# A ranking emitted six wide products later, and the last expert's scatter-adds without an order among them

## The chip, the cores and the metric

The kernel runs on one core of a Trainium2 chip. Its engines are TensorE (PE in the profile; PEld is its weight load), VectorE (DVE), ScalarE (ACT), GpSimd (POOL) and SyncE (SP), and 16 DMA engines. The metric is the device time of one execution in microseconds.

## The reference

Three layers follow each other on 3072 tokens of 384 numbers: a linear attention with decay, a product of two linear maps with two more maps behind it, and a mixture of eight experts of which each token takes two.

```python
for t in range(S):                                   # attention: 4 x 8 heads, 768 steps, 48 wide
    state = alpha[:, :, t, :, None] * state + np.einsum('bhd,bhe->bhde', k[:, :, t], v[:, :, t])
    y[:, :, t] = np.einsum('bhd,bhde->bhe', q[:, :, t], state)
...
h = (x @ w1) * (x @ w2) @ w3                         # x: 3072 x 384, w1, w2: 384 x 1024
x = h @ w_out
...
noisy_logits = x @ w_gate + np.log1p(np.exp(x @ w_noise)) * noise
top2 = np.argpartition(-noisy_logits, 2, axis=1)[:, :2]
for e in range(E):                                   # 8 experts, 384 -> 1024 -> 384
    for k in range(2):
        mask = top2[:, k] == e
        h = np.maximum(x[mask] @ w1[e], 0.0)
        out[mask] += top2_w[mask, k, None] * (h @ w2[e])
```

## The kernel before

**Groups.** The tokens are worked on in eight groups g of 384. For a group the kernel does, in turn, the attention in three chunks, the wide products of the second layer, the narrow products, and the routing. w3 and w_out are multiplied into one matrix beforehand (`Wf`). Factors are held as two half-precision parts, "h" and "l", so a product is three matmuls a block: h by h, h by l, l by h.

**Wide and narrow products.** `wide(g, f, i)` forms block f (of eight) of x @ w1 or x @ w2 (i is 0 or 1): nine matmuls on L531 to L533. ScalarE copies the result (ab), VectorE multiplies the two (L539) and splits the product into gh and gl (L180, L182). So a group has 16 wide products. `narrow(g, t, part)` multiplies gh and gl by `Wf` and the gates (L555 to L557), for three blocks t of 128 tokens in two parts each.

**Attention beside it.** Its steps are woven between these products: scores (L299) with scales of their own (L275 to L289), a mask and a split (sf on L306, sm on L180 and L182, the latter on GpSimd), the mix with the state (L338, L349), the state's own update (L368 on TensorE, Zs on L392 and L393 on VectorE), the turns of the output (ys, L401) and of the inputs (pad, L219), Qt and Kt (L246, L261).

**Routing and ranking.** `route(g, ...)` runs on VectorE and ScalarE behind the narrow products of group g and ends with M, which marks each token's two experts, and the counts of the tokens ahead (M on L644 and L646, R on L647, md on L639 to L641). `rank(g)` turns M into places: two small matmuls (L656, L657), some ten short operations on VectorE (rk on L659 to ad on L682), and six indirect DMAs on GpSimd (L685), which write the tokens' numbers and weights into a table in memory. The first ranking also starts the filling of the output with zeros (`clear`).

**Experts.** Behind the last group each expert e gathers its tokens by the table, takes them through its two layers (L894 to L905, L911 to L916) and adds the results to the output: `put` scales a tile of 128 tokens on ScalarE (ysb, L934) and GpSimd issues an indirect DMA that adds its rows in memory (L935), seven for an expert.

**What sets the order.** TensorE runs in the order in which the program emits its instructions. A loop takes units from two lists, the attention's and `mix_units`, by their costs. On the other engines a scheduler sets the order ahead of time, by when it expects operands. In `mix_units` the ranking of group g-1 is emitted in group g behind block f = RF = 3, that is behind eight wide products. PSUM is used in eight buffers in rotation, one also for each ranking. Two DMAs that touch the same tensor are ordered by a wait unless the program declares that they don't depend on each other; `rank` does so for the table's.

Of the kernel before, what the change touches and what calls it, by code (L numbers as in the profile page):

```python
# [20 lines left out]
P = 128  # L21
# [3 lines left out]
E = 8  # L25
# [5 lines left out]
NG = NTOK // G  # L31
# [8 lines left out]
NTA = G0 // P  # L40
NFR = 2
RF = 3
PA = 1
WB = 12
WU = 3
# [39 lines left out]
def body(ctx, tc, q, k, v, alpha, mw1, mw2, mw3, mwo, wg, wn, noise, ew1, ew2, out, dbg=None):  # L85
    nc = tc.nc
# [678 lines left out]
    def fuse_units():  # L765

        n0 = 4 * NK
        yield 0.33, (lambda: fuse_out_turn(0)), n0 + 1
        for f in range(NF):
            if f + 1 < NF:  # L770
                yield 0.33, (lambda f=f: fuse_out_turn(f + 1)), n0 + f + 2
            yield 0.55, (lambda f=f: fuse_out(f)), 0
        n0 += NF
        seq = [(f, hf) for f in range(NF) for hf in range(2)]
        yield 0.45, (lambda: fuse_turn(*seq[0])), n0 + 1
        for n, x in enumerate(seq):
            if n + 1 < len(seq):
                yield 0.45, (lambda n=n: fuse_turn(*seq[n + 1])), n0 + n + 2
            yield 2.05, (lambda x=x: fuse_mul(*x)), 0
# [16 lines left out]
    def mix_units():  # L796
        fu = fuse_units()
        for g in range(NG):
            for f in range(NF):
                for i in range(2):  # L800
                    if g == 0:
                        yield (0.0, (lambda f=f: convert((f // 4 + 1) * 2 * NK + AH)), TG - 1)
                    yield (1.48, (lambda g=g, f=f, i=i: wide(g, f, i)), (g + 1) * TG - 1)
                    if g == NG - 1 and f > RF:
                        yield (0.0, (lambda: prepare_after(LAST[-1], PA)), 0)
                    if g == 0 and f >= FF:
                        c, x, n = next(fu)
                        yield 0.0, (lambda n=n: convert(n + AH)), 0
                        yield c, x, 0
                if f == RF and g:  # L810
                    yield (0.1, (lambda g=g: LAST.append(rank(g - 1))), 0)
                    if g == NG - 1:
                        yield (0.0, begin_experts, 0)
            if g == 0:
                for c, x, n in fu:
                    yield 0.0, (lambda n=n: convert(n + AH)), 0
                    yield c, x, 0
                yield (0.0, end_of_weights, 0)
            for t in range(TG):
                for part in range(2):  # L820
                    yield (2.05, (lambda g=g, t=t, part=part: narrow(g, t, part)), 0)
                    if g == NG - 1:
                        yield (0.0, (lambda: prepare_after(LAST[-1], PA)), 0)
                        if 0 <= t * 2 + part - T0 < NTP[0]:
                            yield (0.34, (lambda i=t * 2 + part - T0: turn_part(0, 0, i)), 0)
# [78 lines left out]
        nc.scalar.activation(hh[:, f], pm, AF.Relu)  # L904
        nc.vector.scalar_tensor_tensor(hl[:, f], pm, 0.0, hh[:, f], op0=OP.max, op1=OP.subtract)  # L905

    def layer2(w2h, w2l, hh, hl, c0, n, mt, wv, t, midway=None):
        ts = slice(c0, c0 + n)
        py = bank(DM)
        for f in range(NF):  # L910
            nc.tensor.matmul(py[:n], hh[:, f, ts], w2h[:, f], start=f == 0, stop=False)  # L911
            nc.tensor.matmul(py[:n], hh[:, f, ts], w2l[:, f], start=False, stop=False)  # L912
            nc.tensor.matmul(py[:n], hl[:, f, ts], w2h[:, f], start=False, stop=f == NF - 1)  # L913
            if f == 2 and midway:
                midway()
        put(py[:n], n, mt, wv, t)  # L916

    def layer2t(w2h, w2l, hh, hl, c0, n):

# [9 lines left out]
        nc.scalar.activation(yt, py, AF.Copy)  # L929
        return yt  # L930

    def put(py, n, mt, wv, t):
        ys = ep.tile([P, DM], F32, name="ysb", bufs=3)
        nc.scalar.activation(ys[:n], py, AF.Copy, scale=wv[:n, t:t + 1])  # L934
        nc.gpsimd.indirect_dma_start(  # L935
            out=out, out_offset=bass.IndirectOffsetOnAxis(ap=mt[:n, t, 0:1].bitcast(U32), axis=0),
            in_=ys[:n], in_offset=None, compute_op=OP.add)

    def slots(src, n, part):
        mt = ep.tile([P, NTA, 2], F32, name=f"mt{part}")  # L940
# [8 lines left out]
    PARTS = ((0, G0), (G0, CAP))  # L949
    NTP = [-(-(c1 - c0) // P) for c0, c1 in PARTS]  # L950
    EW, EX, EH, WV = {}, {}, {}, {}
    todo = []

    def fetch_part(e, p):
# [17 lines left out]
    def second(e, p, t, midway=None):  # L972
        n = PARTS[p][1] - PARTS[p][0]
        mt = EX[e, p][0]
        if t == 0:
            WV[e, p] = factors(mt, -(-n // P), EW[e][2], EW[e][5], p)
        wv = WV[e, p]
        layer2(EW[e][3], EW[e][4], *EH[e, p], t * P, min(P, n - t * P), mt, wv, t, midway)

    def last_few(e):  # L980

        t, n = NTP[1] - 1, (CAP - G0) % P
        mt = EX[e, 1][0]
        yt = layer2t(EW[e][3], EW[e][4], *EH[e, 1], t * P, n)

        def rest():
            pt = bank(NK, P)
            for k in range(NK):
                nc.tensor.transpose(pt[:n, k, :], yt[:, k, :], ident)  # L989
            put(pt[:n].rearrange("p k d -> p (k d)"), n, mt, WV[e, 1], t)  # L990

        return rest

# [10 lines left out]
    def prepare_after(ins, n):  # L1004
        with tc.issue_after(ins):
            prepare(n)
# [214 lines left out]
```

## Time and profile before

| | |
|---|---|
| median of three runs | 1006.76 us |
| lowest and highest | 1004.91 and 1011.94 us |
| profiled execution | 1014.1 us |
| its span | 1012.2 us |
| TensorE busy | 947.1 us (94%) |
| VectorE busy | 613.5 us (61%) |
| GpSimd busy | 254.0 us (25%) |

The profile is of one execution, a little longer than the median of the runs. Its span begins and ends with the program's own work, and 1.9 us lie around it. Times in rows count from the span's start.

### The profile page before, as it was taken

How to read it: one execution, taken by the hardware profiler on the slowest of the kernel's cores; microseconds unless marked ns; L12 is line 12 of the kernel's file. 1: busy time of each engine (PE TensorE's matmuls, PEld its weight loads, DVE VectorE, ACT ScalarE, POOL GpSimd, SP SyncE). 2: the span in 40 equal slices, each digit the busy share in tenths (PEclk: the TensorE clock that was granted, in tenths of full speed). 3: DMA queues.
4: the chain of work that ended last, by engine and by line, in shares of the span. 5: the costliest groups of instructions: out<-in, count | busy, mean ns of one | idle time of the engine just before them, and what ended most of it. 6: DMA issues, size and time to landing. Idle time of an engine off the chain costs nothing. (4 is left out here: it accounts for less than half of the span.)

```text
span 1012.2 us, 18282 instructions
## 1 busy us (share of the span) xinstructions
PE 947.1 (94%) x7159; PEld 628.9 (62%) x7159; DVE 613.5 (61%) x1696; ACT 498.9 (49%) x972; POOL 254.0 (25%) x246
## 2 busy tenths in 40 slices
PE   7889999999998999899898889999999999999992
PEld 4768777777666665567554446666666565656562
DVE  6698878677687794967464837536272626354210
ACT  3866764454655646545445435444453535354310
POOL 2121110040412122031214062342323324242212
PEclk9788999999999999999999999999999999999997
DMA  9894681436224150002103344454443535342212
GB/s 248 213 164 96 167 211 31 80 95 189 46 49 63 39 86 3 24 1 87 33 24 104 106 105 132 114 126 101 111 118 75 155 64 134 90 107 61 28 17 36
DMA packets 144472, 94.58 MB, mean 93 GB/s; under 512 B 112112, under 2 KB 130112, under 8 KB 144384
## 3 DMA queue, kind: packets, MB, share of 16 engines
q1 hardware_dynamic: 127824, 57.02, 23.9%
q0 software_dynamic: 16560, 36.37, 16.3%
q8 instruction: 57, 0.93, 0.4%
q14 instruction: 31, 0.25, 0.1%
HBM read 73.06 MB, written 20.31 MB: 92 GB/s over the span
## 5 line engine op out<-in xcount | busy, mean ns | idle before, releaser
L935 POOL DMA_INDIRECT out_dram<-ysb,mt x56 | 90.4, 1615 | 265.0 <-ACT ysb L934 131.3
L905 DVE SCALAR_TENSOR_TENSOR hl<-ps,hh 128x512 f16<-128x512 f32 (+1 forms) x128 | 74.5, 587 | 105.1 <-ACT hh L904 99.8
L903 PE MATMUL ps<-xT,el 128*128 128x320 f16 (+1 forms) x384 | 130.9, 341 | 4.8 <-DVE el L184 4.8
L901 PE MATMUL ps<-xT,eh 128*128 128x320 f16 (+1 forms) x384 | 130.7, 340 | 1.3 <-ACT xT L895 1.3
L902 PE MATMUL ps<-xT,eh 128*128 128x320 f16 (+1 forms) x384 | 130.7, 340 | 0.0
L912 PE MATMUL ps<-el,hh 128*128 128x384 f16 x384 | 125.9, 328 | 2.5 <-DVE el L184 2.5
L913 PE MATMUL ps<-eh,hl 128*128 128x384 f16 x384 | 125.8, 328 | 0.0
L911 PE MATMUL ps<-eh,hh 128*128 128x384 f16 x384 | 125.8, 328 | 0.0
L904 ACT ACTIVATE hh<-ps 128x512 f16<-128x512 f32 (+1 forms) x128 | 66.0, 516 | 101.0 <-PE ps L903 84.6
L184 DVE SCALAR_TENSOR_TENSOR el<-es,esc,eh 128x512 f16<-128x512 f32 (+1 forms) x80 | 66.9, 857 | 51.2 <-ACT eh L180 49.7
L934 ACT ACTIVATE ysb<-ps,wv 128x384 f32<-128x384 f32 (+1 forms) x56 | 32.4, 578 | 132.7 <-PE ps L913 67.8
L685 POOL DMA_INDIRECT table<-md,ad x48 | 48.0, 1001 | 152.0 <-DVE ad L682 74.9
L535 ACT ACTIVATE ab<-ps 128x384 f32<-128x384 f32 (+2 forms) x136 | 61.4, 465 | 34.3 <-PE ps L533 23.3
L531 PE MATMUL ps<-xT,w0h 128*128 128x384 f16 (+2 forms) x204 | 67.2, 331 | 2.6 <-DVE Zs L392 1.5
L886 POOL DMA_INDIRECT xg<-x2s,mt x56 | 55.7, 994 | 51.1 <-PE ps L903 19.0
L182 POOL TENSOR_TENSOR sm<-sf,sm 128x512 f16<-128x512 f32 x24 | 28.4, 1201 | 160.0 <-ACT sm L180 159.9
L533 PE MATMUL ps<-xT,w0l 128*128 128x384 f16 (+2 forms) x204 | 67.0, 330 | 1.1 <-issue 1.1
L532 PE MATMUL ps<-xT,w0h 128*128 128x384 f16 (+2 forms) x204 | 67.3, 331 | 0.0
L531 PE MATMUL ps<-xT,w1h 128*128 128x384 f16 (+2 forms) x204 | 66.5, 326 | 0.0
L532 PE MATMUL ps<-xT,w1h 128*128 128x384 f16 (+2 forms) x204 | 66.4, 326 | 0.0
L533 PE MATMUL ps<-xT,w1l 128*128 128x384 f16 (+2 forms) x204 | 66.2, 325 | 0.0
L555 PE MATMUL ps<-Wh,gh 128*128 128x400 f16 x192 | 63.9, 333 | 0.9 <-ACT gh L180 0.9
(288 smaller groups left out, 2175.1 us busy)
## 6 DMA issues: line engine op xcount, KB each, us to landing
es<-in_moe_w_dram SPq DMA_DIRECT2D x32, 768.0 KB
s<-in_moe_w_dram POOLq DMA_DIRECT2D x16, 512.0 KB
out_dram<-zero POOLq DMA_DIRECT2D x5, 960.0 KB
v<-in_v_dram SPq DMA_DIRECT2D x24, 192.0 KB
x2s<-xr SPq DMA_DIRECT2D x24, 192.0 KB
pad<-in_alpha_dram SPq DMA_DIRECT2D x21, 192.0 KB
pad<-in_q_dram SPq DMA_DIRECT2D x21, 192.0 KB
pad<-in_k_dram SPq DMA_DIRECT2D x21, 192.0 KB
```

Source lines behind the costliest of these rows:

```text
L184: nc.vector.scalar_tensor_tensor(lo, src, scale, hi, op0=OP.mult, op1=OP.subtract)
L531: nc.tensor.matmul(pm, wab[i][0][:, kk, fs], xT[:, kk, cs], start=kk == 0, stop=False)
L532: nc.tensor.matmul(pm, wab[i][0][:, kk, fs], xT[:, NK + kk, cs], start=False, stop=False)
L533: nc.tensor.matmul(pm, wab[i][1][:, kk, fs], xT[:, kk, cs], start=False, stop=kk == NK - 1)
L901: nc.tensor.matmul(pm, w1h[:, kk, fs], xT[:, kk, :n], start=kk == 0, stop=False)
L902: nc.tensor.matmul(pm, w1h[:, kk, fs], xT[:, NK + kk, :n], start=False, stop=False)
L903: nc.tensor.matmul(pm, w1l[:, kk, fs], xT[:, kk, :n], start=False, stop=kk == NK - 1)
L905: nc.vector.scalar_tensor_tensor(hl[:, f], pm, 0.0, hh[:, f], op0=OP.max, op1=OP.subtract)
L911: nc.tensor.matmul(py[:n], hh[:, f, ts], w2h[:, f], start=f == 0, stop=False)
L912: nc.tensor.matmul(py[:n], hh[:, f, ts], w2l[:, f], start=False, stop=False)
L913: nc.tensor.matmul(py[:n], hl[:, f, ts], w2h[:, f], start=False, stop=f == NF - 1)
L935: nc.gpsimd.indirect_dma_start(out=out, out_offset=bass.IndirectOffsetOnAxis(ap=mt[:n, t, 0:1].bitcast(U32), axis=0), in_=ys[:n], in_offse ...
```

## The change

Of the eight rankings the six that are emitted in groups 1 to 6 (those of groups 0 to 5, "ranking 0" to "ranking 5") move from behind eight wide products to behind fourteen. The one in group 7 and the one among the experts stay. And the seven scatter-adds of the last expert are declared independent of each other: an expert has each token once, so they write different rows.

```diff
+RG = 6
...
-                if f == RF and g:
+                if f == (RF if g == NG - 1 else RG) and g:
                     yield (0.1, (lambda g=g: LAST.append(rank(g - 1))), 0)
...
-    def layer2(w2h, w2l, hh, hl, c0, n, mt, wv, t, midway=None):
+    def layer2(w2h, w2l, hh, hl, c0, n, mt, wv, t, midway=None, e=None):
...
-        put(py[:n], n, mt, wv, t)
+        put(py[:n], n, mt, wv, t, e)
...
-    def put(py, n, mt, wv, t):
+    def put(py, n, mt, wv, t, e=None):
         ys = ep.tile([P, DM], F32, name="ysb", bufs=3)
         nc.scalar.activation(ys[:n], py, AF.Copy, scale=wv[:n, t:t + 1])
-        nc.gpsimd.indirect_dma_start(
+        i = nc.gpsimd.indirect_dma_start(
             out=out, out_offset=bass.IndirectOffsetOnAxis(ap=mt[:n, t, 0:1].bitcast(U32), axis=0),
             in_=ys[:n], in_offset=None, compute_op=OP.add)
+        if e == E - 1:
+            for o in adds.setdefault(e, []):
+                tc.declare_no_dep(i.ins, o.ins, reason="an expert has each token once")
+            adds[e].append(i)
...
+    adds = {}
```

The line numbers of the new kernel are one to six higher than those of the old one (L656 becomes L657, L935 becomes L936).

On TensorE, in group 5, ranking 4 stood between a mix and the ninth wide product (`before` and `ones` are the constants that count the tokens ahead, in a block and in earlier ones):

```order
L349 MATMUL ps<-vh,sm_5136 128x48
L656 LDWEIGHTS before
L656 MATMUL ps<-M,before 128x24
L657 LDWEIGHTS ones
L657 MATMUL ps<-M,ones 128x24
L531 LDWEIGHTS w0h
L531 MATMUL ps<-xT,w0h 128x384
```

Now, in the same group:

```order
L402 MATMUL ps<-ident_67,ys 128x128
L657 LDWEIGHTS before
L657 MATMUL ps<-M,before 128x24
L658 LDWEIGHTS ones
L658 MATMUL ps<-M,ones 128x24
L300 MATMUL ps<-Qt,Kt 128x128 x8
L532 LDWEIGHTS w0h
L532 MATMUL ps<-xT,w0h 128x384
```

It has moved behind a turn of the output and ahead of the scores of the next chunk, with the last pair of wide products behind these.

On VectorE, in group 6, the work of ranking 5 stood ahead of the state's update:

```order
L672 TENSOR_REDUCE rs<-oh 128x6
L182 TENSOR_TENSOR gl<-ab_6265,gh 128x384
L674 TENSOR_SCALAR ge<-rs 128x6
L676 TENSOR_TENSOR si<-rs,ge 128x6
L677 TENSOR_SCALAR si<-si 128x6
L678 TENSOR_SCALAR si<-si 128x6
L679 SCALAR_TENSOR_TENSOR rs<-si 128x6
L682 TENSOR_TENSOR ad<-rs,rr 128x6
L539 TENSOR_TENSOR ab_6355<-ab_6367,ab_6355 128x384
L182 TENSOR_TENSOR gl<-ab_6355,gh 128x384
L392 SCALAR_TENSOR_TENSOR Zs_120<-ps,scl,Zs_119 48x4x48 x2
L393 TENSOR_TENSOR Zs_120<-Zs_120,Ae 48x4x48 x2
```

Now, at the same update:

```order
L540 TENSOR_TENSOR ab_6331<-ab_6343,ab_6331 128x384
L183 TENSOR_TENSOR gl<-ab_6331,gh 128x384
L393 SCALAR_TENSOR_TENSOR Zs_120<-ps,scl,Zs_119 48x4x48 x2
L394 TENSOR_TENSOR Zs_120<-Zs_120,Ae 48x4x48 x2
L540 TENSOR_TENSOR ab_6360<-ab_6381,ab_6360 128x384
L183 TENSOR_TENSOR gl<-ab_6360,gh 128x384
L176 TENSOR_SCALAR xsc<-xsc 128x1
L177 TENSOR_SCALAR xsc<-xsc 128x1
L178 TENSOR_SCALAR xe<-xsc 128x1
L569 TENSOR_SCALAR xe<-xe,scl 128x3
L185 SCALAR_TENSOR_TENSOR ys<-ps,xsc,ys 128x384
L660 COPY rk<-ps 128x24
```

The ranking's operations (the copy rk is the first) come behind the update of Zs and the split of the output ys.

On GpSimd, at the end of the program, these are the last expert's seven adds with what they wait for (DMASW are the semaphores on which GpSimd's DMAs report their landing, Activation that of ScalarE):

```order
L935 DMA out_dram<-ysb,mt_10923 3200x384 [waits DMASW3_49,DMASW2_49,Activation_49]
L935 DMA out_dram<-ysb,mt_10923 3200x384 [waits DMASW3_49,Activation_49]
L935 DMA out_dram<-ysb,mt_10923 3200x384 [waits DMASW4_49,Activation_49]
L935 DMA out_dram<-ysb,mt_10923 3200x384 [waits DMASW5_49,Activation_49]
L935 DMA out_dram<-ysb,mt_11344 3200x384 [waits DMASW6_49,Activation_49]
L935 DMA out_dram<-ysb,mt_11344 3200x384 [waits DMASW7_49,Activation_49]
L935 DMA out_dram<-ysb,mt_11344 3200x384 [waits DMASW0_49,Activation_49]
```

Now, with the add of the expert before ahead of them and what follows on the engine:

```order
L936 DMA out_dram<-ysb,mt_10768 3200x384 [waits DMASW2_49,DMASW1_49,Activation_49]
L936 DMA out_dram<-ysb,mt_10923 3200x384 [waits DMASW3_49,DMASW2_49,Activation_49]
L936 DMA out_dram<-ysb,mt_10923 3200x384 [waits Activation_49] x3
L936 DMA out_dram<-ysb,mt_11344 3200x384 [waits Activation_49] x3
L1132 TENSOR_LOAD li [waits DVE_49]
```

The first add waits as before; the other six wait for their tile from ScalarE only.

## Rows read from the trace of the kernel before

**Rows 1.** The page: busy time of each engine; the table's DMAs as a group.

```profile
PE 947.1 (94%) x7159; PEld 628.9 (62%) x7159; DVE 613.5 (61%) x1696; ACT 498.9 (49%) x972; POOL 254.0 (25%) x246
...
L685 POOL DMA_INDIRECT table<-md,ad x48 | 48.0, 1001 | 152.0 <-DVE ad L682 74.9
```

**Rows 2.** The chain that ended last: start, duration, what.

```profile
994.82 4.34 DMA out_dram<-ysb,mt
```

**Rows 3.** GpSimd's timeline, last expert: start, duration, instruction, [idle before <-what ended it].

```profile
973.19 1.55 POOL L935 DMA_INDIRECT out_dram<-ysb,mt  x1 [20.95 <-ACT ysb L934]
...
1003.93 1.56 POOL L935 DMA_INDIRECT out_dram<-ysb,mt  x1 [2.60 <-DMA out_dram<-ysb,mt]
```

**Rows 4.** ScalarE's timeline, last expert.

```profile
972.34 0.58 ACT L934 ACTIVATE ysb<-ps,wv 128x384 f32<-128x384 f32 x1 [3.51 <-PE ps L913]
...
991.83 0.57 ACT L934 ACTIVATE ysb<-ps,wv 64x384 f32<-64x384 f32 x1 [1.23 <-PE ps L989]
994.27 0.58 ACT L934 ACTIVATE ysb<-ps,wv 128x384 f32<-128x384 f32 x1 [1.86 <-PEq L1127]
```

**Rows 5.** TensorE's waits in the whole span: total us, times, longest.

```profile
PE ps L657 <- DVE M L646: 5.1, 4, 2.0
...
PE ps L656 <- DVE M L644: 2.2, 2, 2.0
...
PE ps L557 <- DVE gl L182: 0.6, 1, 0.6
```

**Rows 6.** TensorE's timeline behind ranking 1 (first three rows) and ranking 4.

```profile
262.19 0.18 PE L657 MATMUL ps<-M,ones 128*128 128x24 bf16 x1 [1.41 <-DVE M L646]
...
264.95 0.33 PE L531 MATMUL ps<-xT,w1h 128*128 128x384 f16 x1
265.11 0.33 PE L532 MATMUL ps<-xT,w1h 128*128 128x384 f16 x1
...
424.43 0.19 PE L656 MATMUL ps<-M,before 128*128 128x24 bf16 x1 [1.97 <-DVE M L644]
426.59 0.18 PE L657 MATMUL ps<-M,ones 128*128 128x24 bf16 x1 [1.97 <-DVE M L646]
...
432.22 0.33 PE L531 MATMUL ps<-xT,w0h 128*128 128x384 f16 x1
```

**Rows 7.** Timelines of VectorE and of GpSimd ahead of ranking 4.

```profile
423.28 1.10 DVE L644 TENSOR_TENSOR M<-oh 128x24 bf16<-128x24 f32 x1
...
423.15 2.32 POOL L182 TENSOR_TENSOR sm<-sf,sm 128x512 f16<-128x512 f32 x2 [24.24 <-ACT sm L180]
```

**Rows 8.** Windows: us, busy (x instructions) by engine, PEclk (granted clock), DMA share, GB/s.

```profile
425.30:432.10 6.80, 5.51 (x19) 2.64 (x19) 5.02 (x26) 3.23 (x8) 0.84 (x2) 0.50 0.00 0
432.20:438.00 5.80, 5.80 (x45) 4.31 (x43) 2.86 (x5) 2.95 (x6) 4.27 (x6) 1.00 0.02 1
490.10:493.50 3.40, 3.35 (x34) 3.07 (x35) 1.05 (x2) 0.52 (x1) 2.66 (x3) 0.50 0.57 181
```

**Rows 9.** Timelines of VectorE and TensorE at ranking 5 and behind it.

```profile
484.65 0.18 DVE L659 COPY rk<-ps 128x24 f32<-128x24 f32 x1
...
486.68 0.17 DVE L682 TENSOR_TENSOR ad<-rs,rr 128x6 int32<-128x6 f32 x1
...
490.15 2.00 PE L338 MATMUL ps<-Zs,Qt 112*128 112x96 f32 x8 [2.56 <-DVE Zs L393]
```

**Rows 10.** TensorE's timeline behind ranking 2 and at ranking 3.

```profile
314.11 0.34 PE L531 MATMUL ps<-xT,w0h 128*128 128x384 f16 x1 [1.45 <-DVE Zs L392]
...
367.94 0.17 PE L657 MATMUL ps<-M,ones 128*128 128x24 bf16 x1 [0.77 <-DVE M L646]
```

**Rows 11.** TensorE's timeline at the narrow products of group 2.

```profile
283.40 0.34 PE L557 MATMUL ps<-Wh,gl 128*128 128x400 f16 x1 [0.59 <-DVE gl L182]
```

**Rows 12.** Windows at the zero fill and the loads behind it, columns as in rows 8.

```profile
219.00:238.00 19.00, 19.00 (x139) 12.95 (x138) 15.14 (x38) 7.98 (x19) 5.39 (x6) 1.00 0.93 278
...
250.00:260.40 10.40, 10.40 (x89) 7.82 (x87) 10.24 (x53) 5.77 (x13) 1.16 (x1) 1.00 0.86 153
```

More of the change, by code (lines that the diff above doesn't have):

```diff
@@ L977, in second @@
         wv = WV[e, p]
-        layer2(EW[e][3], EW[e][4], *EH[e, p], t * P, min(P, n - t * P), mt, wv, t, midway)
+        layer2(EW[e][3], EW[e][4], *EH[e, p], t * P, min(P, n - t * P), mt, wv, t, midway, e)
     def last_few(e):
@@ L989, in rest @@
                 nc.tensor.transpose(pt[:n, k, :], yt[:, k, :], ident)
-            put(pt[:n].rearrange("p k d -> p (k d)"), n, mt, WV[e, 1], t)
+            put(pt[:n].rearrange("p k d -> p (k d)"), n, mt, WV[e, 1], t, e)
         return rest
```

## The prediction

> **What bounds the kernel now.** I read the page first. TensorE is busy 94% of the span, VectorE 61% [rows 1], so time comes off in two ways only: where TensorE waits or runs at the lower clock, and after its last instruction. The chain that ended last says where the second lies: behind TensorE's end it is one scatter-add after another, each with a landing of up to 4.3 us [rows 2]. GpSimd's timeline shows the seven adds of the last expert between 973.19 and 1003.93, and what the last of them waited for is the landing of the one before [rows 3]; so do the others behind the first. Their inputs are there long before: ScalarE ends the last of the seven tiles at 994.27 + 0.58 = 994.85 [rows 4]. So the adds, not TensorE, set the end.
>
> For the first way I read TensorE's waits by what ended them. The two matmuls of a ranking stand in the list with 5.1 us and 2.2 us, and two waits for the state's Zs lie near rankings too [rows 5, 9, 10]. Then I looked at each of the six rankings that move, with the stretch behind it, because the granted clock falls behind three of them: 0.50 in 425.3 to 432.1 and in 490.1 to 493.5 [rows 8], and nine wide matmuls from 262.2 to 264.95, 0.30 us apart, where the next start 0.16 apart [rows 6]. Experts follow from 584 on and keep TensorE busy, so what is won ahead of them should arrive at the end.
>
> **The adds.** Removed: six waits for a landing. The first add still waits as before; the others wait for ScalarE alone, as the order shows. ScalarE to GpSimd took 973.19 - (972.34 + 0.58) = 0.27 us [rows 3, 4]. An add holds GpSimd 1.56 us, and the last two tiles, which come closest, are 2.4 us apart [rows 4], so GpSimd doesn't queue. The last add begins at 994.85 + 0.27 = 995.12 in place of 1003.93: **8.8 us**. What comes behind it, 1012.2 - 1003.93 = 8.3 us, stays. An add of 4.3 us meets the next one 2.4 us later at worst; if the two couldn't overlap at all, 1.9 us would be lost. Bounds 6.9 to 8.8; I take 8.8, since the adds that now follow closely are few and small.
>
> **The six rankings.** Each adds nothing and takes nothing away; it moves behind six more wide products. One of those is nine matmuls 0.16 us apart, so TensorE comes to the ranking at least 6 x 9 x 0.16 = 8.6 us later. What M needs is finished at the old place at most 2.0 us late [rows 5, 7], so the wait for M goes in all six. What a ranking brings with it are some ten short operations on VectorE, 484.65 to 486.85 in the fifth with two others between them, some 1.8 us by themselves [rows 9], and six indirect DMAs on GpSimd. These now stand ahead of other work. The splits that GpSimd does for the scores move ahead of the DMAs instead of behind; the mix that reads a split comes an iteration later, so I cost that at nothing; with that cover gone it would cost up to six issues of 1.0 us [rows 1]. SP's order is unchanged. Numbers below are the group whose ranking it is.
>
> Ranking 4: TensorE waits 1.97 us for M twice, then runs 18 wide matmuls in 432.22 - 426.61 = 5.6 us (the first starts 0.02 behind the row at 426.59) at half clock, for which full clock takes 18 x 0.16 = 2.9 [rows 6, 8]. Together 3.9 + 2.7 = 6.6 us. The clock fell behind this idling, and I see nothing else ahead of it. VectorE was late since additions of its chain took 1.1 us beside two GpSimd splits of 2.32 us together [rows 7]; their like take 0.17 [rows 9]. In the new place VectorE is busy 2.86 of 5.80 us [rows 8], room for 1.8. But the new place is amid the scale chain of the scores, and VectorE's waiting work ends no sooner, so something of the wait may come back. Bounds 3.9 to 6.6; I take **5.5**.
>
> Ranking 5: no wait for M. Its VectorE work stands ahead of ab, gl and then Zs; TensorE waits 2.56 us for Zs and then has half clock for 3.4 us, 1.7 lost [rows 8, 9]. In the new order that work stands behind Zs. Zs would be ready 1.8 us sooner; the wait might be 0.7 and the clock stay up, or another wait keep it down. Bounds 0 to 4.3. I take **1.0**, near the lower end, since the 1.8 us are less than the wait of 2.56 and so a gap, with its clock, likely remains.
>
> Ranking 1: 1.41 us for M and nine matmuls in 2.74 us instead of 1.47 [rows 6]: 2.7 in all. Against it, the narrow products of this group wait 0.59 us for gl already [rows 11], and the ranking's VectorE work comes just ahead of that, so that 1.8 us may return. Bounds 0 to 2.7; I take **1.0**.
>
> Ranking 3: 0.24 and 0.77 us of waiting; 0.77 stands in its row and 0.24 is the rest of the 2.2 us [rows 5, 10]. Bounds 0 to 1.0; I take **1.0**, as no later stall of that group waits for VectorE's ranking work.
>
> Ranking 2: none for M, but the next wide product waits 1.45 us for Zs, and the nearest reason is a PSUM buffer that the ranking takes in rotation [rows 10]. It could come free; the scores next in line need VectorE anyhow. Bounds -1.0 to 1.45; I take 0.
>
> Ranking 0: no wait. It starts the zero fill of the output, 219 to 238, when the DMA engines are 93% busy; behind the move that fill falls on 233 to 253, and from 250 to 260.4 they are 86% busy with the next loads [rows 12]. If the loads come late, ScalarE's use of them is late. Bounds -3.0 (an estimate: the overlap, 3 us of fill) to 0; I take 0.
>
> **The sum.** 5.5 + 1.0 + 1.0 + 1.0 = 8.5 (bounds -0.1 to 16.0) and 8.8, so 17.3 us. The profiled execution took 1014.1 us, 1.9 more than its span; it would come to 996.8. It lies 7.3 us above the median of the runs, 1006.76. The same 17.3 taken off the median gives **989.5 us**.
>
> **The Trainium skill.** The addition at 423.28 takes 1.10 us on VectorE while GpSimd runs splits [rows 7]. The Trainium skill (SBUF — State Buffer, section Who interferes with whom) says that a VectorE instruction with two SBUF inputs contends with a GpSimd instruction that reads SBUF, while a reduction doesn't. The row agrees. By that rule the moved rankings are in danger wherever splits stand near them in the new order: three of a ranking's operations are of that sort, and each would take some 0.9 us more, by the row, so at most 2.8 us for a ranking and 16.6 us for six. That speaks against this change, and it would make the third rival below worse by that.
>
> **Rivals.** *Only the adds pay.* VectorE is the late engine in this stage, and TensorE, freed of the wait at the ranking, meets it at the scores, the mix or the narrow products. For it: waits for Zs and gl [rows 9, 11]. Against: VectorE has half its time free right behind ranking 4. Then 1006.76 - 8.8 = 998.0.
>
> *The adds still follow one another,* because landings of close adds lengthen or the order isn't what binds. For: they write rows of one tensor over the same DMA engines. Against: the last add's wait ends at a landing [rows 3], and in the new order it waits for ScalarE alone. Then 1006.76 - 8.5 = 998.3.
>
> *Slower.* The ranking's work on VectorE, 1.8 us, now stands just ahead of the last gl of the group, for which the narrow products wait 0.59 already in one group [rows 11]. If gl has less than 1.8 us of room in all six groups, TensorE waits 1.8 us and falls to half clock, 1.7 us lost as behind the Zs wait of [rows 9], in each: 6 x 3.5 = 21.0 us. It decides from 17.3 / 3.5, that is from five groups on. Then 1006.76 - 17.3 + 21.0 = 1010.5. Against: the list has this wait for gl once only, 0.6 us in all [rows 5], and attention work stands between a ranking and the narrow products.
>
> **How the numbers follow.** The forecast has 0.70: its range, by the bounds, is 982 to 996.5. Only the adds: 0.16, 995.5 to 1001, a third of it below 996.7. The adds in sequence: 0.07, half of it below. Slower: 0.07, half of it over 1016.8. About 1%, 10 us, is what tells a change from none here, so faster means under 996.7: 0.70 + 0.05 + 0.03 = 0.78; slower 0.03; within 1% the other 0.19. For 8 in 10 I go from 982 to 1000; beyond it lie 0.07 below and some 0.12 above.
>
> **What the new profile would show.** Seven adds at the tail some 0.3 us behind their tiles, the last starting about 8.3 us ahead of the span's end; no wait of the ranking's matmuls for M in groups 1 to 6; full clock where ranking 4's stretch was at half; the Zs wait behind ranking 5 under 1 us; at the narrow products of each group a wait for gl of under 0.6 us. I'd be wrong if waits for gl or Zs of 1.5 us and more with half clock appear in groups that have none now, if the loads behind the zero fill land late, or if adds take over 6 us to land.

## The result, and the profile after

| | before | after |
|---|---|---|
| median | 1007.09 us (4 runs, 1004.91 to 1011.94) | 997.91 us (4 runs, 994.98 to 1000.7) |
| profiled execution | 1014.1 us | 1000.15 us |
| its span | 1012.2 us | 998.2 us |

The ratio is 0.9915, with a 95% interval from 0.9891 to 0.994: 9.2 us less between the medians, where 17.3 were forecast. The time lies outside the forecast's range of 982 to 996.5 us (that range doesn't reach as far as the prediction's own bounds do: 1006.76 - 6.9 + 0.1 = 1000), though within the 982 to 1000 to which it gave 8 in 10. The gain is clear of noise, about half of the one forecast, and within the 10 us that the forecast called no change. The number is that of the first two rivals, 998.0 and 998.3, but by another sum, as the runs below show. In a later batch the same kernel against the same kernel before gave 13.2 us, 0.9872 [0.9843, 0.9901] (it is `e5_again` below); the two intervals overlap, so the gain is known to some 4 us only.

The page's first line of the changed kernel shows the same work:

```profile
PE 943.4 (95%) x7159; PEld 624.8 (63%) x7159; DVE 615.6 (62%) x1696; ACT 496.9 (50%) x972; POOL 253.8 (25%) x246
```

**The adds did what was forecast.** GpSimd's timeline of the changed kernel at the end (start, duration, instruction, idle before and what ended it), against [rows 3]:

```profile
968.03 1.55 POOL L936 DMA_INDIRECT out_dram<-ysb,mt  x1 [20.77 <-ACT ysb L935]
971.93 1.55 POOL L936 DMA_INDIRECT out_dram<-ysb,mt  x1 [2.35 <-ACT ysb L935]
...
989.96 1.56 POOL L936 DMA_INDIRECT out_dram<-ysb,mt  x1 [1.02 <-ACT ysb L935]
```

ScalarE's timeline there, against [rows 4]:

```profile
989.11 0.58 ACT L935 ACTIVATE ysb<-ps,wv 128x384 f32<-128x384 f32 x1 [1.86 <-PEq L1133]
```

The releaser has changed from a landing to ScalarE. The last add starts 989.96 - 989.11 = 0.85 us behind the start of its tile's scaling, as the first does in [rows 3, 4] (973.19 - 972.34), and 998.2 - 989.96 = 8.2 us ahead of the end, as before (8.3). Between the last tile and the last add lay 1003.93 - 994.27 = 9.66 us, now 0.85: 8.8 us. The seven landings took 3.3 to 4.4 us; six of before, in its chain that ended last, 3.27 to 4.38.

**The waits at rankings are gone,** all but one that isn't moved. TensorE's waits in the changed kernel, against [rows 5] (total, times, longest):

```profile
PE ps L300 <- DVE Kt L247: 6.7, 7, 2.0
...
PE ps L402 <- ACT ab L536: 2.0, 1, 2.0
PE ps L339 <- DVE Zs L394: 1.9, 1, 1.9
...
PE ps L658 <- DVE M L647: 1.0, 1, 1.0
...
PE ps L558 <- DVE gl L183: 0.6, 1, 0.6
```

The ranking's first matmul (now L657) isn't in the list any more, and its second (L658) has one wait of 1.0 us, at the ranking that stayed in group 7. Of the waits for M, 5.1 + 2.2 us before, 1.0 is left. The stretch around ranking 4, against [rows 6]:

```profile
436.01 0.49 PE L402 MATMUL ps<-ident,ys 128*128 128x128 f16 x6
436.35 0.18 PE L657 MATMUL ps<-M,before 128*128 128x24 bf16 x1
436.37 0.17 PE L658 MATMUL ps<-M,ones 128*128 128x24 bf16 x1
437.24 0.94 PE L300 MATMUL ps<-Qt,Kt 48*128 48x128 f32 x12 [0.69 <-DVE Zs L393]
```

No wait for M is left; 0.69 us of one for Zs stands behind it.

**But a wait came up that wasn't there,** in group 2 behind the first ranking's new place. TensorE's timeline of the changed kernel:

```profile
252.41 0.17 PE L276 MATMUL ps<-ss,ones 128*128 128x5 bf16 x1
254.57 0.49 PE L402 MATMUL ps<-ident,ys 128*128 128x128 f16 x6 [1.99 <-ACT ab L536]
255.50 0.32 PE L532 MATMUL ps<-xT,w1h 128*128 128x384 f16 x1 [0.43 <-DVE Kt L247]
...
259.98 0.49 PE L300 MATMUL ps<-Qt,Kt 48*128 48x128 f32 x4 [2.00 <-DVE Kt L247]
```

That is 4.4 us of waiting within 7.5 us. The windows, against [rows 12]:

```profile
232.90:250.00 17.10, 17.10 (x132) 12.20 (x130) 9.51 (x34) 7.06 (x17) 5.47 (x6) 1.00 0.98 303
250.00:260.40 10.40, 5.98 (x50) 4.03 (x48) 6.07 (x25) 2.97 (x6) 0.00 (x0) 1.00 0.76 182
260.90:264.30 3.40, 3.40 (x14) 1.68 (x12) 3.40 (x22) 2.43 (x6) 0.00 (x0) 0.55 1.44 157
```

The zero fill now keeps the DMA engines 98% busy from 232.9 to 250, TensorE is busy 5.98 of the 10.4 us behind it, where it was busy all the time [rows 12], and the granted clock then falls to 0.55 for 3.4 us. ScalarE's timeline names what it was late for:

```profile
247.81 0.53 ACT L181 ACTIVATE gh<-ab 128x384 f16<-128x384 f32 x1 [1.18 <-DVE ab L540]
253.53 0.61 ACT L181 ACTIVATE xr<-x,am 128x384 f16<-128x384 f32 x1 [5.19 <-DMA x2s<-xr]
254.04 0.85 ACT L536 ACTIVATE ab<-ps 128x384 f32<-128x384 f32 x2
```

VectorE's timeline has the split's second half, which waits for the first:

```profile
254.17 0.62 DVE L185 SCALAR_TENSOR_TENSOR xr<-x,am,xr 128x384 f16<-128x384 f32 x1 [5.12 <-ACT xr L181]
```

xr is the tile of a block of routed tokens on its way to memory. It has two buffers, a group stores three blocks, so the third waits until the first store has landed, and that store lies behind the zero fill: issued at 245.5, it landed 7.9 us later (the tile's view ends with "DMA to landing us min/median/max: 2.2/7.9/7.9"). ScalarE stands for 5.19 us and the copies of the wide products (ab, L536) queue behind it; VectorE stands for 5.12 us and Kt (L247) comes behind it; TensorE waits for ab and for Kt. SyncE, which issues the third store and then the loads of q and k, begins with the loads at 255.7 instead of 250.2, so the loads come late as well, one of the signs that the prediction named. The profile of before has the row that tells this; it isn't among the rows that the prediction reads (SyncE's timeline of the kernel before, three stores):

```profile
245.16 4.40 SPq L582 DMA_DIRECT2D x2s<-xr  x3
```

It stands right in the 233 to 253 to which the prediction moved the fill.

### The profile page after: what moved, and what is told of

Its sections match the earlier page's. It is cut to its first block, busy times and chain, and to the rows that moved or that the text cites. A ratio compares the mean times of both kernels' runs of the same rounds, so it can differ in the third digit from the quotient of the medians.

```text
span 998.2 us, 18279 instructions
## 1 busy us (share of the span) xinstructions
PE 943.4 (95%) x7159; PEld 624.8 (63%) x7159; DVE 615.6 (62%) x1696; ACT 496.9 (50%) x972; POOL 253.8 (25%) x246
## 5 line engine op out<-in xcount | busy, mean ns | idle before, releaser
L936 POOL DMA_INDIRECT out_dram<-ysb,mt x56 | 90.3, 1613 | 256.6 <-ACT ysb L935 137.8
L935 ACT ACTIVATE ysb<-ps,wv 128x384 f32<-128x384 f32 (+1 forms) x56 | 32.4, 578 | 132.9 <-PE ps L914 71.0
L536 ACT ACTIVATE ab<-ps 128x384 f32<-128x384 f32 (+2 forms) x136 | 61.4, 466 | 21.1 <-PE ps L534 19.8
L532 PE MATMUL ps<-xT,w0h 128*128 128x384 f16 (+2 forms) x204 | 65.7, 323 | 1.1 <-ACT xT L403 1.1
L181 ACT ACTIVATE gh<-ab 128x384 f16<-128x384 f32 (+2 forms) x68 | 34.4, 507 | 64.3 <-DVE ab L540 63.9
```

The source lines that it names most:

```text
L532: nc.tensor.matmul(pm, wab[i][0][:, kk, fs], xT[:, kk, cs], start=kk == 0, stop=False)
L936: i = nc.gpsimd.indirect_dma_start(out=out, out_offset=bass.IndirectOffsetOnAxis(ap=mt[:n, t, 0:1].bitcast(U32), axis=0), in_=ys[:n], in_o ...
```

## The experiments

All comparisons are between kernels with the same work, unless said otherwise. Kernels of a batch ran on one chip with the kernel before.

To see which group a microsecond belongs to, I took from TensorE's timeline the start of the first narrow product of every group, and the differences. The column of group g runs from group g-1's narrow products to group g's and holds the wide products of group g with ranking g-1 among them:

| kernel | group 2 | group 3 | group 4 | group 5 | group 6 |
|---|---|---|---|---|---|
| before | 54.62 | 54.17 | 56.43 | 57.63 | 52.42 |
| before, second trace (e11) | 53.33 | 54.58 | 52.45 | 57.54 | 52.45 |
| adds alone (e1) | 53.37 | 53.61 | 52.48 | 58.71 | 52.44 |
| after | 58.45 | 52.28 | 53.23 | 54.05 | 51.93 |
| after, second trace (e5) | 58.86 | 52.29 | 53.21 | 54.04 | 52.08 |
| rankings alone (e2) | 56.72 | 52.24 | 53.22 | 54.08 | 51.87 |
| ranking 0 stays (e3) | 51.77 | 52.48 | 53.20 | 54.09 | 51.92 |
| the same again (e10) | 51.78 | 52.46 | 53.26 | 55.71 | 51.84 |
| fill at its old time (e6) | 51.78 | 52.49 | 53.28 | 54.06 | 51.91 |
| three buffers for xr (e4) | 51.78 | 55.61 | 53.19 | 55.81 | 51.84 |
| rankings 1 to 5 behind ten (e7) | 53.18 | 53.52 | 50.99 | 56.11 | 53.79 |
| ranking 4 alone moved (e8) | 55.04 | 53.64 | 56.31 | 52.11 | 51.20 |
| ranking 3 behind ten (e9) | 51.78 | 52.45 | 53.13 | 55.77 | 50.27 |
| rankings 1 to 5 behind twelve (e12) | 51.78 | 56.58 | 51.63 | 54.64 | 50.27 |

For instance the second narrow start of "after" is 224.17 and the third 282.62, a difference of 58.45. The columns leave out what stands ahead of the first narrow product, which starts between 166.94 and 173.22 us in the 14 traces, though no edit changes anything ahead of it; this spread is in the runs' times.

### The two halves of the change

`e1_adds_only`: the changed kernel with all rankings at the old place.

```diff
-RG = 6
+RG = 3
```

> The last expert's adds unordered, all rankings at the old place. Theory A (the adds give what the trace shows, 8.8 us, whatever happens ahead of them): 1007.1 - 8.8 = 998.3 us, the last add 8.3 us ahead of the span's end. Theory B (the six rankings gave the 9 us that the runs show and the adds little): over 1003 us.

Measured: 997.95 us (5 runs, 995.62 to 999.4), 0.9898 [0.988, 0.9915] of the 1006.97 of the kernel before. That is 9.0 us: theory A.

`e2_ranks_only`: the rankings moved, the adds in order.

```diff
-        if e == E - 1:
+        if e == E:
```

> The six rankings moved, the adds ordered as before. Theory A (the two traces put side by side: the rankings of groups 1 to 5 win some 12 us and the one of group 0 loses some 6.5, 5.3 in all): 1001.8 us. Theory B (the traces mislead, since the profiled execution of before is 7 us above its median; the rankings win nothing, 9.2 - 8.8 = 0.4 us): 1006.7 us.

Measured: 1001.98 us (6 runs), 0.9949 [0.9931, 0.9966], 5.0 us: theory A. So the adds give their 8.8 us (e1), and it is the rankings that fell short: 5.0 in place of 8.5. In this trace ScalarE's wait for xr in group 2 is 5.1 us too. The agreement with 1001.8 is in part luck: theory A's 12 and 6.5 us were taken from the first trace of before, and by the traces below the parts are 6.9 and 4.9. By the runs the halves add up to 14.0 us, nearer to the 13.2 of e5 than to the 9.2 of the result.

### What ranking 0 takes along

`e3_rank0_stays`: the whole change, but the ranking emitted in group 1 stays behind eight wide products, and the zero fill with it.

```diff
-                if f == (RF if g == NG - 1 else RG) and g:
+                if f == (RF if g in (1, NG - 1) else RG) and g:
```

> The whole change, but ranking 0, and with it the zero fill, stays behind eight wide products. Theory A (the fill's new place costs TensorE a wait of 4.4 us in group 2 and 1.7 us of half clock behind it): the wait at 252.6 to 255 and at 258 to 260 is gone, 997.9 - 6.1 = 991.8 us. Theory C (the wait is due to the VectorE work that stands in another order in groups 1 and 2, and it would come back elsewhere): 997 to 999 us.

Measured: 991.38 us (5 runs, 990.41 to 992.26), 0.9839 [0.9824, 0.9855]: theory A. Group 2 takes 51.77 us in place of 58.45, the other groups as in the changed kernel. This is 15.6 us below the kernel before, near the 17.3 forecast for the whole.

`e6_fill_old_place`: all six rankings moved, and the fill started by itself behind the twelfth wide product of group 1.

```diff
-        with tc.issue_after(scat[0].ins):
-            nc.gpsimd.memset(zero, 0.0)
+        if True:
+            x = AB[0][:, :DM // 2]
+            nc.gpsimd.tensor_tensor(zero, x, x, OP.subtract)
...
-        if g == 0:
-            clear()
...
+                if g == 1 and f == 5:
+                    yield (0.0, clear, 0)
                 if f == (RF if g == NG - 1 else RG) and g:
```

> The whole change, all six rankings moved, but the zero fill is started by itself at about its old time (218 us): its tile of zeros is a product of the twelfth wide product's pair less itself, formed on GpSimd, in place of a fill with a constant behind the ranking's DMAs. Theory A (the fill alone is what ranking 0 takes along): as with ranking 0 at its old place, 990.5 to 993 us, no wait of over 1 us in group 2 before 262. Theory C (ranking 0's own work on VectorE and TensorE does it): 995 to 998 us, the wait in group 2 as before.

`e5_again`: the changed kernel unedited, beside it on the same chip.

> The changed kernel as it is, beside the others on one chip. If its group 2 waits by chance for as long as the zero fill holds the stores up, its runs spread over some 5 us (995 to 1000.7 so far), with a median of 995 to 998 us and a wait of 2 to 4.5 us in group 2.

Measured, against 1012.88 us of the kernel before on that chip: e5 999.67 us (6 runs, 995.54 to 1003.55), 0.9872 [0.9843, 0.9901]; e6 994.19 us (5 runs, 993.59 to 996.3), 0.9812 [0.9791, 0.9832]. e6's median lies a little above the band that was expected, on a chip on which the kernel before was slower; against e5 beside it, it is 5.5 us less. Ranking 0 itself is at its new place in e6, with the same order on TensorE and VectorE as in e5. So the fill makes the difference, not the ranking's own work: theory A. In e6 the fill is on GpSimd's timeline at the old time, ahead of the table's DMAs:

```profile
219.00 4.75 POOL L519 DMA_DIRECT2D out_dram<-zero  x5 [0.30 <-POOL zero L516]
```

In group 2 of e6 no wait of TensorE is left (its list of waits from 226 to 282 is empty), and group 2 takes 51.78 us. e5 has the wait again; these are ScalarE's and TensorE's rows of it from the two lists of waits:

```profile
ACT xr L181 <- DMA x2s<-xr: 5.6, 1, 5.6
...
PE ps L402 <- ACT ab L536: 2.4, 1, 2.4
PE ps L300 <- DVE Kt L247: 2.0, 1, 2.0
```

`e4_xr3`: the changed kernel, the fill where the change puts it, but the stored tile from three buffers of its own in all groups but the last two.

```diff
-            xr = sp.tile([P, 2, DM], F16, name="xr")
+            xr = (late.tile([P, 2, DM], F16, name="xrf", bufs=3) if g < NG - 2 else
+                  sp.tile([P, 2, DM], F16, name="xr"))
```

> The whole change, and the tiles xr of the routed tokens, in all groups but the last two, come from three buffers of their own, so that ScalarE's third split needn't wait until the first store of xr has landed behind the zero fill. Theory A1 (this wait of ScalarE, 5.2 us at 248.3 to 253.5, is how the fill reaches TensorE): 997.9 - 6.1 = 991.8 us, with the fill where the change puts it. Theory A2 (the loads of q and k behind the fill are late as well and TensorE waits for them instead): 994 to 998 us, with waits for pad in group 2.

Measured: 994.98 us (5 runs, 993.14 to 998.33), 0.9885 [0.9864, 0.9906]. Both theories hold a part. Group 2 takes 51.78 us, as short as with the fill out of the way: the wait for xr's buffer is the whole of how the fill reached TensorE there (A1). But group 3 takes 55.61 in place of 52.5. ScalarE's timeline of e4 shows why the fill isn't free yet:

```profile
261.70 1.16 ACT L262 ACTIVATE Kt<-pad 128x1152 f32<-128x1152 f32 x1 [1.73 <-DMA pad<-in_k_dram]
```

The load of k is late by 1.7 us, and TensorE meets that at the narrow products of group 2 (a wait of 1.6 us for gh at 280.4, behind which the clock falls to 0.83 in the ten us from 280). That is A2's late load, with ScalarE and not TensorE waiting for it, and the mechanism for which the prediction had bounds. The 3.1 us are near the 3.0 of its bound by luck: that was an overlap of transfers, and this is 1.4 us of later arrival and a fall of the clock that costs 1.7. That the late load leads to the wait 19 us behind it is read from the order of ScalarE's work; no run moves the load by itself. The median is 3.6 us above that of e3 on the same chip.

### The other five rankings

`e8_rank4_only`: adds unordered, only the ranking in group 5 moved.

```diff
+                if f == (RG if g == 5 else RF) and g:
```

> Adds unordered and ranking 4 alone moved, the other rankings at their old places. By the traces of the kernels with the adds alone and with ranking 0 staying, group 5 is 4.6 us shorter: 998.0 - 4.6 = 993.4 us. By the prediction's 5.5: 992.5 us. If the gain of the five rankings is spread evenly (6.6 in all): 996.7 us.

Measured: 997.03 us (5 runs, 996.07 to 997.61), 0.9841 [0.982, 0.9862], on the slower chip. The expected times were worked out from another chip's, where the kernel before had 1007; this median can't be set against them. On its own chip it is 2.8 us above e6, which has all the other rankings moved as well. In its trace group 5 takes 52.11 us, 5.4 to 6.6 less than in the three traces with ranking 4 at the old place, about what was forecast; but group 4 takes 56.31, with stops in the mix (1.1 us) like those of the first trace of before (1.9). Groups 4 and 5 together take 108.42 us there, 109.99 in e11, 111.19 in e1 and 107.29 in e3: ranking 4 alone wins 1.6 to 2.8 us of the sum in this one trace, rankings 3 and 4 win 2.7 to 3.9. A stop in one group may give VectorE and ScalarE time to catch up, which the next group then has; that is argued, not tried.

`e7_four_later` and `e12_five`: ranking 0 stays, rankings 1 to 5 behind ten and behind twelve wide products.

```diff
-RG = 6
+RG = 4
...
-                if f == (RF if g == NG - 1 else RG) and g:
+                if f == (RF if g in (1, NG - 1) else RG) and g:
```

(5 in place of 4 for e12.)

> Adds unordered, ranking 0 at its old place, rankings 1 to 5 behind ten wide products instead of fourteen. Theory D (what counts is that M is ready; it is 2.0 us late at most, and two wide products with what stands between them take over 3 us): 990.5 to 992.5 us. Theory E (six products are needed, since the ranking's VectorE work still stands ahead of Zs and ab there): 994 to 998 us.

> Adds unordered, ranking 0 at its old place, rankings 1 to 5 behind twelve wide products. If what matters is only that M is ready and the VectorE work of a ranking has room anywhere behind: as behind fourteen, within 1 us. If the place among the group's other work matters: up to 4 us more, as behind ten, with waits for Zs or gh in other groups than there.

Measured: e7 997.68 us (5 runs), 0.9852 [0.9827, 0.9877] on the slower chip, 3.5 above e6 there. e12 991.47 us (5 runs), 0.9853 [0.9829, 0.9877], against e10's 992.0 in the same rounds. Behind ten, M isn't ready in time for ranking 4, and the wait for Zs behind ranking 5 is 2.3 us, against 1.9 behind fourteen (TensorE's list of waits of e7, 220 to 500):

```profile
PE ps L339 <- DVE Zs L394: 2.3, 1, 2.3
...
PE ps L658 <- DVE M L647: 1.2, 1, 1.2
```

So theory D falls, and E's time holds for ten. Twelve is as good as fourteen in the sum, though not for the reason in the first case of its expectation: groups 4 and 6 are 1.6 us shorter than in e10, and the column of group 3 is 4.1 longer, since at its beginning the narrow products of group 2, behind ranking 1, wait for the last gl (TensorE's waits of e12, 274 to 284):

```profile
PE ps L558 <- DVE gl L183: 3.0, 1, 3.0
```

It looks like the mechanism of the prediction's third rival, but it isn't: the ranking's work on VectorE ended at 269.6, 11 us ahead of that gl. What stands ahead of gl is one short copy (e12, VectorE, then GpSimd):

```profile
276.87 2.77 DVE L234 COPY sm<-A 128x3 f32<-128x3 f32 x1
...
276.35 0.96 POOL L686 DMA_INDIRECT table<-md,ad  x1 [0.31 <-issue]
277.34 2.27 POOL L183 TENSOR_TENSOR sm<-sf,sm 128x512 f16<-128x512 f32 x2
```

Such a copy takes 0.17 us where no split runs beside it. Here it ends when GpSimd's two splits end, and these stand behind the six DMAs of ranking 1, which hold GpSimd until 277.3. More of this stands below, where ranking 3 is accounted for.

Group 6 is shorter for another reason. In e9 too it takes 50.27 us, with ranking 5 behind fourteen as in e10. The wait for Zs is 1.9 us in all of them; the clock stayed full behind it in e9 and e12 and fell in e10.

`e9_mixed`: for each group the best place so far, ranking 3 behind ten.

```diff
-                if f == (RF if g == NG - 1 else RG) and g:
+                if f == {1: 3, 4: 4, 7: 3}.get(g, RG) and g:
```

> Adds unordered; ranking 0 at its old place, ranking 3 behind ten wide products, rankings 1, 2, 4 and 5 behind fourteen: for each group the place at which its traces were shortest so far (group 4: 50.99 us behind ten, 53.20 behind fourteen). If the groups' times add up whatever the neighbours do: 2.2 us less than with ranking 3 behind fourteen, in the same rounds. If group 5 gives it back, as it did when all rankings stood behind ten (56.1 in place of 54.1): the same time.

`e10_rank0_stays_again`: e3 on the same chip as e9.

> Adds unordered, ranking 0 at its old place, rankings 1 to 5 behind fourteen: 15 to 19 us below the kernel before, whichever of the two levels (1007 or 1013 us) that has on this chip, and 5.5 us below what the changed kernel had against it.

Measured, against 1007.01 us: e9 992.14 us (6 runs, 988.63 to 997.64), 0.9858 [0.983, 0.9886]; e10 992.0 us (5 runs, 988.59 to 993.88), 0.9854 [0.9832, 0.9876]. The mix wins nothing. Group 4 takes 53.13 us in e9, not the 50.99 of e7, with ranking 3 at the same place in both: its shortness came with where the neighbours' rankings stood. Group 5 takes 55.77, as the expectation's second case has it: a split on VectorE (gl, 382.89) takes 3.08 us there instead of 0.55, beside GpSimd's splits behind ranking 3's DMAs. e10 is 15.0 us below the kernel before, at the near edge of what was expected. The second half of its expectation stays open: its gain is 5.8 us more than that of the result (9.2) and 1.8 more than that of e5 (13.2), each on another chip or on one that isn't on record. The 5.5 us rest on e5 and e6 side by side.

### The kernel before once more

`e11_before_again`: no edit.

> The kernel before, for a second trace of it. If its waits at rankings are the same in every execution, the list has about 7 us for M again, 2.5 for Zs behind ranking 5, and the stretches of half clock behind them. If the profile of before was a bad execution, some of them are gone, the stop of 1.9 us in the mix of group 4 first, and the time is 1005 to 1008 us.

Measured: 1007.32 us (12 runs, 1004.5 to 1010.78), 1.0002 [0.9986, 1.0017]. Both halves of the expectation hold, each in its part. The waits at rankings are the same in this trace (TensorE's waits, 200 to 560), as in [rows 5, 9]:

```profile
PE ps L657 <- DVE M L646: 5.1, 4, 1.9
PE ps L338 <- DVE Zs L393: 2.5, 1, 2.5
...
PE ps L656 <- DVE M L644: 2.2, 2, 2.0
```

The stop in the mix of group 4 is gone: group 4 takes 52.45 us where the first trace had 56.43. The half clock behind ranking 1 [rows 6] is gone as well, though the wait of 1.4 us ahead of it is there (group 2: 53.33, not 54.62); that behind rankings 4 and 5 is there again. So some 5 us of the profiled 1014.1 us came with that execution or its chip: of the other traces only e8, on the slower chip, has the long group 4. The prediction did not count that stop for ranking 3. No trace with ranking 3 moved has it, but nor have two of the four with ranking 3 at its old place, so whether the two belong together is open.

## Why the prediction came out at half

**The adds** were priced at 8.8 us and gave 8.8 by the traces and 9.0 in the runs. Close adds didn't lengthen each other's landing so far that the end moved: from the last add to the end it is 8.2 us, as before, and the longest landing is 4.4 us. The second rival falls. (In the trace of before one of the six waits, of 4.81 us ahead of the add at 984.57, doesn't end at a landing as the prediction says of all; the sum doesn't use it.)

**Rankings 1 to 5** were priced at 8.5 us together. From the second trace of before to e3 they gave, group by group, 1.6, 2.1, -0.8, 3.5 and 0.5: 6.9 us, and 998.0 - 991.4 = 6.6 in the runs on one chip (e1 against e3).
- Ranking 1: 1.0 forecast, 1.6. The half clock that the prediction counted for it was that of one execution (e11 and e1 have none there).
- Ranking 2: 0 forecast, 2.1 in this pair of traces, outside the bound of 1.45, and 1.1 in the pair e1 and e3. The wait of 1.45 us in [rows 10] did belong to the ranking (1.99 in e11, 0.25 in e3).
- Ranking 3: 1.0 forecast, -0.8. The two waits for M, 0.22 and 0.77 us in e11, went, but TensorE, there sooner, meets two others (timeline of e3; e11 has none of the first kind and 0.67 of the second):

```profile
367.58 0.32 PE L532 MATMUL ps<-xT,w1h 128*128 128x384 f16 x1 [1.53 <-ACT ab L536]
374.97 0.49 PE L300 MATMUL ps<-Qt,Kt 48*128 48x128 f32 x4 [0.96 <-DVE Kt L247]
```

  Ahead of these stands a second term that the prediction put at nothing. It said that GpSimd's splits for the scores move ahead of a ranking's DMAs. In group 4 they come behind the six DMAs of ranking 2, which hold GpSimd from 336.8 to 344.4, and a short copy on VectorE takes 2.29 us beside the splits, where one 1.2 us ahead of it took 0.17 (timelines of the changed kernel, GpSimd, then VectorE):

```profile
343.46 0.96 POOL L686 DMA_INDIRECT table<-md,ad  x1 [0.30 <-issue]
344.44 2.28 POOL L183 TENSOR_TENSOR sm<-sf,sm 128x512 f16<-128x512 f32 x2
...
343.25 0.17 DVE L234 COPY sm<-A 128x3 f32<-128x3 f32 x1 [1.99 <-ACT A L229]
344.46 2.29 DVE L234 COPY sm<-A 128x3 f32<-128x3 f32 x1
```

  The copy takes 2.3 us in all eight traces with ranking 2 behind fourteen, 1.1 behind twelve (e12), and isn't lengthened behind ten or eight. Group 4 goes with it: 53.1 to 53.3 us with ranking 2 behind fourteen, whether ranking 3 stands behind fourteen or behind ten (e9), 51.6 behind twelve, 51.0 behind ten. So what the column books on ranking 3 is by these traces some 2 us that ranking 2 costs in the next group. No run takes the splits or the DMAs away, so that is read and not tried.

- Ranking 4: 5.5 forecast, 3.5, and 4.6 from e1 to e3. Its waits went, and so did the half clock (1.00 in the windows from 420 to 460 of the changed kernel). Of the 3.9 us of waiting 2.4 came back in the same group, for ab, Zs and Kt (timeline of e3):

```profile
426.21 1.03 PE L369 MATMUL ps<-v,ks 128*112 128x96 f32 x8 [1.07 <-ACT ab L536]
431.92 0.94 PE L300 MATMUL ps<-Qt,Kt 48*128 48x128 f32 x12 [0.70 <-DVE Zs L393]
433.51 0.49 PE L300 MATMUL ps<-Qt,Kt 48*128 48x128 f32 x4 [0.65 <-DVE Kt L247]
```

  "Something of the wait may come back" was right and priced too low.
- Ranking 5: 1.0 forecast, 0.5. The wait for Zs fell from 2.56 to 1.9 us, not under 1: taking 1.8 us of VectorE's work from ahead of Zs gave 0.6 of it, and behind the wait that was left the clock still fell in seven of the eight traces with ranking 5 behind fourteen. The reason that the prediction gave for its low figure, a gap that remains with its clock, was right.

So the first rival's mechanism, TensorE meeting the late VectorE and ScalarE at the next place, is at work in groups 4 and 5, where some 4 us of waiting came back, and little of it in the others.

**Ranking 0** is the step that failed: a term put at nothing. "If the loads come late, ScalarE's use of them is late. Bounds -3.0 (an estimate: the overlap, 3 us of fill) to 0; I take 0." Group 2 lost 56.72 - 51.78 = 4.9 to 58.86 - 51.78 = 7.1 us in the three traces with the fill at its new time, and the runs on one chip 5.5 us (e5 against e6). The collision of the fill with other transfers was seen; the wrong transfer was looked at. What the fill held up first weren't the loads from 250 on but the stores of xr at 245, whose buffer ScalarE needs; e4 takes that wait away and group 2 is short again, and only then the loads' delay appears, with its 3 us. The bound was the overlap of the fill with a window, where the price is that of a landing: the store issued while the fill held the DMA engines 98% busy landed 7.9 us later, in e3, without the fill there, 1.9. Worse, a 0 was taken for a term whose rows showed the DMA engines 93% and 86% busy in the two stretches that were moved onto each other. The size is less sure than the mechanism: e2 against e1 and e3 leaves only 6.6 - 5.0 = 1.6 us for ranking 0 by the medians, with intervals of some 2 us on each of the two differences.

In sum by traces: 8.8 + 6.9 - 4.9 to 7.1 = 8.6 to 10.8 us, and 9.2 were measured, 13.2 in e5. With the fill at its old time the change gives 15.0, 15.6 and 18.7 us on three chips (e10, e3, e6), within 2.3 us of the forecast. So the 998 us of the rival *only the adds pay* came out for another reason: the adds paid, five rankings paid 6.6 to 6.9 us, and the fill took most of that back.

**The rule on the shared ports** (the Trainium skill, SBUF — State Buffer, section Who interferes with whom) showed up once on a ranking's own operations in the changed kernel: ranking 1's first one with two inputs took 0.89 us in place of 0.21, beside two splits on GpSimd (VectorE's row, then GpSimd's):

```profile
278.84 0.89 DVE L671 TENSOR_TENSOR oh<-oh,rk 128x48 f32<-128x48 f32 x1
...
278.51 2.27 POOL L183 TENSOR_TENSOR sm<-sf,sm 128x512 f16<-128x512 f32 x2 [11.09 <-ACT sm L181]
```

A reduction behind it (L673) took its usual 0.20, as the rule says. Of the operations at risk in the six moved rankings (the prediction counts three in each; L680, with two inputs too, is a fourth) this is the only one that was lengthened; its 0.7 us are far from the 16.6 of the worst case. The lengthening that cost more, that of the copy with one input above, isn't in the prediction's reckoning: it looked at the rankings' own operations, not at those that the shifted splits meet. No experiment took the splits away, so what they cost this kernel in all is open.

**Slower** (the third rival) didn't happen: the wait for gl is 0.6 us, once, as before. Of the signs of the new profile, the adds, the waits for M, the full clock at ranking 4 and the waits for gl came as said; the wait for Zs behind ranking 5 stayed over 1 us, and the loads behind the fill came late.

## What to carry to other kernels

A step that is moved brings along every transfer that it starts. Ask of each not only which loads it meets at the new time, but which stores, and how many buffers stand behind them: a store that can't land stops the engine that fills its buffer, and that engine stops the rest. A price to begin with is the time to landing of a transfer that is issued behind the moved one (here 7.9 us, of which ScalarE felt 5.2). Ask the same of the engine that issues them: here six DMA issues of 1.0 us pushed GpSimd's next work onto an operation of VectorE that then took 2.3 us instead of 0.17.

Where adds into one tensor are known to touch different rows, saying so at the very end of a program is worth the sum of the landings that hang there, and that can be read from two rows: 8.8 us here, 9.0 in the runs.

Waits read off one trace are a poor measure of what their removal wins: at ranking 4 TensorE came sooner to the next results of the engines that were late, and 2.4 of 3.9 us came back; at ranking 2 a wait of 1.45 us gave 1.1 to 2.1. And groups aren't independent: a mix of each group's best place won nothing.

## What the hardware showed that was not expected

The granted clock doesn't follow from the waits alone. e3 and e10 are the same program, and from the narrow products of group 4 to those of group 5 their lists of TensorE's waits are the same row by row (1.5, 1.1, 0.7 and 0.6 us). Yet that stretch took 54.09 us in one and 55.71 in the other. The window around the first of these waits, e3 first:

```profile
387.00:390.40 3.40, 1.85 (x21) 1.28 (x23) 1.39 (x5) 3.33 (x12) 2.49 (x4) 1.00 0.02 1
390.40:395.00 4.60, 4.60 (x34) 2.81 (x33) 1.29 (x2) 1.94 (x4) 3.98 (x5) 1.00 0.02 1
```

and e10:

```profile
383.00:386.40 3.40, 2.77 (x25) 2.10 (x25) 0.74 (x3) 3.16 (x9) 2.57 (x3) 0.80 0.02 1
386.40:391.00 4.60, 4.60 (x23) 2.36 (x22) 1.29 (x2) 1.23 (x2) 4.18 (x4) 0.78 0.02 1
```

After the same wait of 1.5 us the clock fell to half for some 3.4 us in one execution (0.80 and 0.78 as means of two windows that it straddles) and stayed full in the other. The fall cost 1.6 us here. It isn't the only pair: behind ranking 1 it fell in the first trace of before and not in e11, after the same 1.4 us, and behind ranking 5 it fell in e10 and not in e9, after the same 1.9. A half-clock stretch seen in one profile is therefore a cost with a chance, and a wait that is taken away should take that chance along (argued, not tried). It is why a forecast made on one trace of before (1014.1 us) should be checked against a second. The larger part of the spread between executions lies elsewhere: between e3 and e10 the first narrow product moved from 171.90 to 166.94 us, and the mean granted clock of the first 166 us was 0.92 and 0.94; in e6, where that product starts last, at 173.22, it was 0.89.

Chips differ too. On one, the kernel before took 1012.88 us (1010.68 to 1015.94, 11 runs), on two others 1007.0; the changed kernel took 999.67 there. From the narrow products of group 7 to TensorE's end the traces on that chip take 455.1 to 456.2 us and those on the others 452.3 to 452.6, for the same instructions; nearly all of the difference arises in the first 140 us of that stretch. The two traces of the result, whose chips aren't on record, show the slower one's length, 455.0 and 455.1. Why is open. It is the reason why kernels are compared here within a batch only.
